# Taps' weights of a convolution read into one partition and spread over all 128 by TensorE

## Chip, cores, metric

One core of a Trainium2 chip runs the whole program. The metric is device time in microseconds, from the start to the end of the program, as a median over runs.

## What is computed

```python
# x [8, 4224, 192], weight [8 heads, 7 taps], all float32
w = exp(weight - max(weight)); w = w / (sum(w) + 1e-09)      # softmax over the 7 taps
y[b, s, h, g] = sum_k w[h, k] * x_pad[b, s + k, h, g]        # causal convolution, 24 columns a head
wq, wk = y @ moe_w_q, y @ moe_w_k                            # 192 -> 64
mixed = (wq @ wk^T / 8) @ y                                  # done as wq @ (wk^T y)
out = relu(mixed) @ moe_w_out                                # 192 -> 192
```

## The kernel before

There are 8 batches of 33 chunks of 128 rows. A batch of x is loaded in four pieces (five in batch 0) of 4 to 9 chunks by DMAs that GpSimd issues (`gen_load`, L543); they turn float32 into bfloat16 on the way, into a ring of three slots, so a load of batch b waits until the convolutions of batch b - 3 have read their slot. The convolution (`gen_conv`, L567) is a product with banded matrices `BAND` that hold the taps, 64 rows at a time; it runs in groups of chunks, five in batch 0 (one per piece) and two in each later batch, and each group in four pairs of heads. ScalarE or VectorE evicts each pair from PSUM into Y. VectorE transposes Y, TensorE makes the Gram matrix of Y and from it, with the weights `w_k`, the small matrix of the mix; `w_q` is applied to the transposed Y. Then come four units a batch: mix, `rl` and `rh` (relu into RT), `f_lo` and `f_hi` (the product with `w_out`), two output copies, and a store of 768 KB that SP issues.

Before all this lies the making of `BAND`. SP issues the load of the 8 x 7 weights (`load_w`, L359): 128 descriptors of 224 bytes, the same row on each of 128 partitions of WT_F. VectorE takes the maximum (`mx`, L441) and subtracts it (`sub`, L442), adds a mask for each partition's own tap (`mine`, L447), ScalarE takes the exponentials (`exp`, L457), VectorE sums them (`sm`, L458), takes the reciprocal (`rc`, L463), multiplies (`wn`, L464) and lays the products out (`taps`, L465). TensorE spreads them into two PSUM banks (`spread`, L478), and two copies (L498) bring them to BAND. Meanwhile TensorE runs filler products of 512 columns on zeros: four (`warm`, L421) that wait only for VectorE to have zeroed RUNUP, then a turn of the matrix `step` (`turned`, L426), then nine (`warm_2`, L430), which stand ahead of the spreading in its queue.

The other weights come by DMAs of SP: `w_out` (WF, L381) next after the taps, W32F (`load_32`, L378: `w_q` again, as 32 rows of 3 x 128), then `w_k` (L380) and `w_q` (L379), each in two DMAs. Four casts (L511) make W32 from W32F, one for each quarter of the partitions, on any of three engines; `casts_k` (L520) make among others the two halves of WKT, both on GpSimd, and `casts_q` (L515) one piece there.

The order is written out by hand in PLAN (L19): each entry is an operation's number (in the order in which the code adds them), its engine (P TensorE, A ScalarE, D VectorE, G GpSimd, S SP), a PSUM bank for a product, a variant, or, behind S, a second operation that SP waits for before it issues. Each engine takes its entries strictly in this order. Semaphore waits follow from what an operation needs (`Program.place`, L165).

Of the kernel before, what the change touches and what calls it, by code (L numbers as in the profile page):

```python
# [25 lines left out]
205P4 200P 206P 207D 202P0 201A 196P6 203P 197P 471G 131P3 204A 212P2 198D 132A 136P0 469G 137P3 139A 42D 148P6 150D  # L26
159P7 147P4 213P 43G 138A 149D 468G 214P 161A 372G 143P0 210D 144Pz 145A 140P3 371G 151P6 208D 152Px 141Px 153A 158P0x
215P 142D 160A 219P5 211D 154P3 155Px 283P0 156D 157S57 170P6 172A 284P 216P 220D 217P 285A 292P3 209D 286P6 293P 287P
218A 162P0 288D 294A 163Pz 223P5 164A 165P2 224D 166P 167D 298P4 169P0 171A 304P6 299P 295P2 300D 305P 296P 176P0y
# [188 lines left out]
def bass_lightweight_conv__then__hypermixer_token_mlp_kernel(  # L218
# [760 lines left out]
```

## Time and profile before

| | us |
|---|---|
| Median of 3 runs | 155.1 (153.89, 155.1, 156.55) |
| Profiled execution | 153.99 |
| Its span, first to last instruction | 152.1 |
| TensorE busy | 140.6 |
| VectorE busy | 119.5 |
| ScalarE busy | 110.6 |
| GpSimd busy | 31.0 |

The profiled execution is 1.9 us longer than its span, and stands 1.1 us below the median, close to the fastest of the three runs. Times in the rows below are counted from the start of the span. PE is TensorE, PEld its weight loads, DVE VectorE, ACT ScalarE, POOL GpSimd, SPq the DMA queue of SP; L345 and L329 are helpers that issue all products, so products are told apart by their tiles: `runup` is a filler, `ident,step` the turn, `taps,stept` the spreading, `xw,band` a convolution.

### The profile page before, as it was taken

To read this page: it belongs to the slowest core of one execution; us is meant where nothing else is said; L and a number is where in the kernel's file an instruction comes from. 1 tells how busy PE (TensorE), PEld (TensorE's weight loads), DVE (VectorE), ACT (ScalarE), POOL (GpSimd) and SP (SyncE) were. 2 spreads that over 40 slices of the span, in tenths; PEclk is the share of its full clock that TensorE was granted. 3 is DMA by queue.
4 is the path that set the end of the run, shared out by engine and by line. 5 is a ranking of instruction groups with operands and counts; after the bars stand their busy time and mean duration, and the time that the engine had idled before them with its cause. 6 is when DMAs were issued, how large, how long until landed. Compare 5 with 4: busy or idle time off the path is not lost.

```text
span 152.1 us, 5602 instructions
## 1 busy us (share of the span) xinstructions
PE 140.6 (92%) x2528; PEld 96.8 (64%) x2528; DVE 119.5 (79%) x165; ACT 110.6 (73%) x167; POOL 31.0 (20%) x41
## 2 busy tenths in 40 slices
PE   5977998999999999999999999999999999999920
PEld 2354745876666876785668766866667577965610
DVE  2659857998898898989988885899799978859500
ACT  0683648778768963798869886979399877989940
POOL 6935932900190007100360000000000000000000
PEclk9999999999999999999999999999999999999985
DMA  2999999999999999999999999999940899899994
GB/s 39 167 186 190 192 192 190 193 191 214 274 193 196 188 194 296 356 342 324 339 338 343 334 269 334 196 188 317 402 165 4 329 382 384 317 387 382 350 383 159
DMA packets 45336, 39.62 MB, mean 260 GB/s; under 512 B 35552, under 2 KB 37376, under 8 KB 45312
## 3 DMA queue, kind: packets, MB, share of 16 engines
q0 software_dynamic: 34320, 12.98, 71.4%
q1 hardware_dynamic: 10992, 26.28, 47.1%
q8 instruction: 20, 0.33, 0.8%
q14 instruction: 4, 0.03, 0.1%
HBM read 26.28 MB, written 25.95 MB: 343 GB/s over the span
## 4 chain that ended last, share of the span: by engine, by line
PE 77%; DMA 13%; DVE 2%; ACT 1%; POOL 1%; issue 1%; SPq 0%; POOLq 0%
PE ps L345 53%; PE ps L329 23%; DMA xw<-in_x_dram 10%; DMA wf<-in_moe_w_k_dram 3%; DVE out_sb L317 1%; PE ps L341 1%; ACT out_sb L317 1%; DVE rt L767 1%; POOL xw L550 1%; SPq L369 0%; POOL wkt L317 0%; POOL ident L402 0%; POOLq L402 0%; POOLq L964 0%
## 5 line engine op out<-in xcount | busy, mean ns | idle before, releaser
L550 POOL DMA_DIRECT2D xw<-in_x_dram x33 | 29.9, 919 | 42.6 <-PE ps L345 41.8
L766 ACT ACTIVATE rt<-ps 128x1024 bf16<-128x1024 f32 (+1 forms) x40 | 31.6, 826 | 6.7 <-PE ps L345 6.4
L345 PE MATMUL ps<-wol,rt 64*128 64x192 bf16 (+1 forms) x372 | 35.9, 246 | 0.0
L329 PE MATMUL ps<-xw,band 64*64 64x408 bf16 (+4 forms) x144 | 32.0, 303 | 2.5 <-DMA xw<-in_x_dram 0.5
L345 PE MATMUL ps<-xw,band 64*64 64x408 bf16 (+4 forms) x464 | 33.6, 316 | 0.0
L317 ACT CAST y<-ps 128x816 bf16<-128x816 f32 (+4 forms) x42 | 29.0, 705 | 6.3 <-PE ps L345 5.2
L317 DVE CAST y<-ps 128x768 bf16<-128x768 f32 (+4 forms) x34 | 28.9, 863 | 3.8 <-PE ps L345 3.3
L317 ACT COPY out_sb<-ps 128x768 f32<-128x768 f32 x36 | 28.5, 801 | 4.4 <-PE ps L345 3.6
L345 PE MATMUL ps<-y 128*64 128x64 bf16 (+1 forms) x528 | 30.8, 222 | 0.2 <-DVE y L317 0.2
L628 DVE STREAM_TRANSPOSE t<-y 128x768 uint32<-128x768 uint32 (+2 forms) x32 | 29.8, 959 | 1.4 <-ACT y L317 0.9
L345 PEld LDWEIGHTS ps<-y 128*64 128x64 bf16 (+1 forms) x528 | 26.0, 105 | 7.3 <-issue 6.3
L317 DVE COPY out_sb<-ps 128x768 f32<-128x768 f32 x28 | 26.6, 957 | 4.9 <-PE ps L345 4.0
L345 PEld LDWEIGHTS ps<-wol,rt 64*128 64x128 bf16 (+1 forms) x372 | 24.1, 115 | 3.0 <-ACT rt L766 0.9
L767 DVE TENSOR_SCALAR rt<-ps 128x512 bf16<-128x512 f32 (+1 forms) x24 | 21.5, 931 | 5.0 <-PE ps L345 4.9
L345 PEld LDWEIGHTS ps<-xw,band 64*64 64x64 bf16 x464 | 14.2, 103 | 12.4 <-issue 6.7
L345 PE MATMUL ps<-woh,rt 64*128 64x192 bf16 (+1 forms) x228 | 21.9, 253 | 0.1
L317 ACT CAST wqt<-ps 128x1024 bf16<-128x1024 f32 x12 | 11.8, 1014 | 11.7 <-PE ps L345 11.7
L345 PE MATMUL ps<-wqt,msb 64*64 64x512 bf16 (+1 forms) x133 | 16.9, 385 | 0.0
L326 PEld LDWEIGHTS <-band 64*64 64x64 bf16 x144 | 13.9, 105 | 3.2 <-issue 0.7
L345 PEld LDWEIGHTS ps<-woh,rt 64*128 64x128 bf16 (+1 forms) x228 | 12.9, 119 | 3.7 <-ACT rt L766 1.1
L329 PE MATMUL ps<-wol,rt 64*128 64x192 bf16 (+1 forms) x56 | 13.4, 246 | 0.2
L329 PE MATMUL ps<-wqt,msb 64*64 64x512 bf16 (+1 forms) x33 | 12.5, 384 | 0.0
(96 smaller groups left out, 118.8 us busy)
## 6 DMA issues: line engine op xcount, KB each, us to landing
out_dram<-out_sb SPq DMA_DIRECT2D x31, 768.0 KB, 8.0
xw<-in_x_dram POOLq DMA_DIRECT2D x24, 384.0 KB, 15.6
xw<-in_x_dram POOLq DMA_DIRECT2D x7, 432.0 KB, 15.2
out_dram<-outl SPq DMA_DIRECT2D x4, 192.0 KB, 5.3
out_dram<-out_sb SPq DMA_DIRECT2D x2, 384.0 KB, 4.9
xw<-in_x_dram POOLq DMA_DIRECT2D x1, 240.0 KB, 5.5
xw<-in_x_dram POOLq DMA_DIRECT2D x1, 192.0 KB, 5.0
wf<-in_moe_w_out_dram SPq DMA_DIRECT2D x1, 96.0 KB, 3.3
```

Of the source, the lines that this page charges most:

```text
L317: return lambda e, op: e.copy(dst(op), src(op)) if op.engine == "ACT" else e.tensor_copy(dst(op), src(op))
L326: e.ldweights(l, tile_position=place)
L329: return e.add_instruction(mybir.InstMatmult(name=nc.get_next_instruction_name(), engine=mybir.EngineType.PE, ins=[e.lower_ap(r), e.lower_ ...
L341: last = e.transpose(o, l, r)
L345: last = e.matmul(o, l, r, start=start, stop=stop, skip_group_check=True, tile_position=at[0] if at else None)
L550: "load", "POOL", lambda e, op: e.dma_start(dst, src), n * 128 * D * 4,
L628: lambda e, op: e.transpose(T[:, yb, c0 : c0 + n, :].rearrange("p c d -> p (c d)").bitcast(U32), Y[:, yb, c0 : c0 + n, :].rearrange("p c d ...
L766: return e.activation(dst(op), src(op), AF.Relu)
L767: return e.tensor_scalar(dst(op), src(op), 0.0, None, op0=ALU.max)
```

## The change

The load of the weights now puts one row of 224 bytes into one partition. A new memset on VectorE makes a row of 128 ones. A new product `on_all`, float32, one row deep, 128 by 56, lays the weights on all 128 partitions of a PSUM bank; it waits for the load and stands behind the turn of `step`. `mx` and `sub` read the weights there, and `sub` gives the bank back.

Two operations more shift the numbers in PLAN: 5 to 24 become 6 to 25, and all from 25 on rise by two. The order is for the most part the old one under new numbers. By engine, with old numbers, these entries moved:

- TensorE: `on_all` between the turn and the nine fillers; a few neighbours swapped (61 ahead of 59 and 76 in batch 0); in the last unit but one and the last, other variants of `f_lo` and `f_hi`, and the pair for the second half ahead of that for the first.
- VectorE: the zeroing of RUNUP is its first instruction, where it was the third. The zeroing of WKB moved from first place to batch 1. One of the four casts of W32F (old 40, new 42) stands between `mine` and `sm`; it stood behind the first eviction. The order around it is now `mx`, `own`, a memset, `sub`, two memsets, `mine`, cast, `sm`.
- The second copy to BAND went from VectorE to ScalarE. In the first two groups of batch 0 VectorE makes four evictions and ScalarE four, where ScalarE had six.
- Between the first 24 us and the last 12, sixteen pieces of work went from ScalarE to VectorE or the other way. In the last two units one large `rl` and two output copies went to VectorE and one output copy to ScalarE.
- GpSimd: loads 180, 181, 182, 183 (batch 1) and 279 to 282 (batch 2) in their natural order ahead of both casts of WKT (47, 46); they were 180, 181, 183, cast, 182, 281, 280, cast, 279. Loads of later batches swap places; five of them stand behind the cast of `w_q` (43), where three did.
- SP: `w_k` waits for the third load of batch 0 instead of the second, `w_q` for the first load of batch 2 instead of the second of batch 1. The first store to go out is that of the last chunks of batches 0 and 1, where it was one of batch 0.

```diff
@@ -17,46 +17,46 @@
 
 
 PLAN = """
-0S 13D 10D 4S 6D 18P4 53G 5D 1S 16G 17D 54G 22D 19P 25D 21P0 55G 26D 7D 20A 56G 23D 11D 27D 28A 8D 24D 57G 41A 9D 29D
-37A 30D 31D 180G 32D 33P1 52A 49A 34D 35P5 181G 58P6 3S54 36D 59P 60A 183G 76P0 70P2 61P4 77P 62P 63D 71P 78A 67P6
-79P0 72A 68P 40D 50A 64P2 80P 69A 73P4 81D 65P 74P 66A 85P6 75A 88P0 39A 91P2 86P 87D 82P4 92P 89P 83P 84A 122P7 14D
-90D 93D 94P0 100P2 119D 95P 101P 102A 103P5 104P 96D 97P0 105A 47G 118D 109P3 182G 98P 99D 110P 111A 106P5 123P 281G
-15D 120D 38A 112P2 51A 107P 115P0 108A 113P 116P 280G 114D 124P 117A 121D 45A 46G 125P 279G 126P 48D 2S181 133P0 135A
-134D 369G 282G 127P 190P4 370G 191P 193P2 128A 187P0 192D 194P 195A 184P6 188P 129P4 44D 12D 185P 189D 199P2 130A 186A
...
-803A 807S660 819P2 816Py 817D 821A 812P0 813Px 830P4x 823P2y 814A 818S749 824Py 825D 832A 826P6 827P 837P4 828A
-829S749 838P 834P6 839A 835Pz 841S 836A 840S750
+0S 7D 19P5 9D 4S 11D 55G 6D 5D 1S 17G 18D 56G 20P 23D 26P1 24D 22P0 27D 57G 25D 8D 21A 28D 58G 12D 10D 29D 30A 42D 31D
+59G 39A 32D 33D 182G 34D 35P7 40A 36D 37P5 38A 60P6 183G 50A 63P4 61P 62D 72P2 184G 78P0 73P 74A 79P 64P 69P6 80D 81P0
+65A 185G 70P 71A 66P2 75P4 82P 83D 3S57 67P 76P 87P6 68A 90P0 43D 281G 51A 93P2 77D 88P 89A 84P4 94P 91P 92D 85P 282G
+124P7 86A 95D 52A 96P0 41A 283G 102P2 121D 97P 54A 103P 53A 105P5 106P 104A 284G 98D 99P0 107A 15D 120D 111P3 100P
+101A 112P 108P5 125P 122D 113A 114P2 117P0 109P 110A 115P 118P 116D 126P 49G 119A 123D 127P 48G 372G 128P 46D 16D 14D
+135P0 137A 136D 373G 371G 129P 192P4 193P 195P2 194A 189P0 130D 196P 47D 190P 191D 186P6 197A 131P5 187P 132A 201P2
...
+818P 823D 814P0 815Px 816A 825P2 819D 820S660 832P4 826P 834A 828P0y 829Py 830D 827A 839P2y 831S749 836P5 837Px 838A
+842S562 840Py 841D 843S751
 """.split()
...
@@ -264,7 +264,8 @@
     def semaphore(name):
         return es.enter_context(nc.semaphore(name))
 
-    WT_F = sbuf("wt_f", [128, H, KC], F32)
+    WT_F = sbuf("wt_f", [1, H * KC], F32)
+    ONES = sbuf("ones", [1, 128], F32)
     WMX = sbuf("wmx", [128, H], F32)
     WEX = sbuf("wex", [128, 2, H, 8], F32)
     WSM = sbuf("wsm", [128, 2, H], F32)
@@ -358,8 +359,8 @@
 
     load_w = add(
         "load_w", "SP",
-        lambda e, op: e.dma_start(WT_F[:, :, :], bass.AP(w_t, 0, [[0, 128], [1, H * KC]])),
-        28000, dma=("w", semaphore("s_w"), 16), vt=-10)
+        lambda e, op: e.dma_start(WT_F[:, :], bass.AP(w_t, 0, [[H * KC, 1], [1, H * KC]])),
+        1000, dma=("w", semaphore("s_w"), 16), vt=-10)
 
     QS, KS, OS = slice(0, DH), slice(DH, 2 * DH), slice(2 * DH, 2 * DH + D)
 
@@ -383,6 +384,7 @@
     def dve(emit, ns, needs=(), vt=0.0, kind="setup"):
         return add(kind, "DVE", emit, ns, needs=needs, vt=vt, info={"ns": ns})
 
+    ones = dve(lambda e, op: e.memset(ONES[:, :], 1.0), 100, vt=-9.6)
     one = dve(lambda e, op: e.memset(IDENT[:, :], 1.0), 165, vt=-9.5)
     zero_r = dve(lambda e, op: e.memset(RUNUP[:, :].bitcast(U32), 0), 270, vt=-9.45)
     zero_s = dve(lambda e, op: e.memset(STEPT[:, :].bitcast(U32), 0), 130, vt=-8.9)
@@ -438,12 +440,22 @@
         lambda e, op: e.tensor_reduce(OWN[:, :], IDENT[:, :].rearrange("p (k i) -> p i k", i=16), AX.X, ALU.add),
         290, needs=[ident], vt=-8.92)
 
-    mx = dve(lambda e, op: e.tensor_reduce(WMX[:, :], WT_F[:, :, :], AX.X, ALU.max), 200, needs=[load_w], vt=-9.3)
-    sub = dve(
+
+    def spread_w(op):
+        yield bank(op.bank)[:, 0 : H * KC], ONES[:, :], WT_F[:, :], True, True, False
+
+    on_all = pe("setup", spread_w, needs=[load_w, ones], after=[turned], banks=1, vt=-9)
+
+    def w_all():
+        return bank(on_all.bank)[:, 0 : H * KC].rearrange("p (h k) -> p h k", k=KC)
+
+    mx = dve(lambda e, op: e.tensor_reduce(WMX[:, :], w_all(), AX.X, ALU.max), 230, needs=[on_all], vt=-9.3)
+    sub = add(
+        "setup", "DVE",
         lambda e, op: e.tensor_tensor(
-            WEX[:, 0, :, 0:KC], WT_F[:, :, :], WMX[:, :].unsqueeze(2).to_broadcast([128, H, KC]), ALU.subtract
+            WEX[:, 0, :, 0:KC], w_all(), WMX[:, :].unsqueeze(2).to_broadcast([128, H, KC]), ALU.subtract
         ),
-        210, needs=[mx], vt=-9.29)
+        230, needs=[mx], drains=on_all, vt=-9.29, info={"ns": 230})
     mine = dve(
         lambda e, op: e.tensor_tensor(
             WEX[:, 1, :, 0:KC], WEX[:, 0, :, 0:KC], OTHER[:, 0:KC].unsqueeze(1).to_broadcast([128, H, KC]), ALU.add
```

## Rows read from the trace of the kernel before

**Rows 1.** The page: busy us, share of the span, instructions of TensorE, VectorE, ScalarE.

```profile
PE 140.6 (92%) x2528; PEld 96.8 (64%) x2528; DVE 119.5 (79%) x165; ACT 110.6 (73%) x167; POOL 31.0 (20%) x41
```

**Rows 2.** The chain that ended last, to 24 us: start, us, what.

```profile
8.10 5.15 DMA wf<-in_moe_w_k_dram
...
13.55 10.21 DMA xw<-in_x_dram
...
23.80 0.32 PE ps L329
```

**Rows 3.** Busy time of each engine by stretch; behind it clock, DMA share, GB/s.

```profile
8.12:23.27 15.15, 13.76 (x307) 9.02 (x308) 11.22 (x22) 8.47 (x22) 7.60 (x10) 1.00 1.58 190
23.27:140.00 116.73, 115.46 (x2121) 82.26 (x2121) 101.69 (x122) 93.22 (x135) 16.54 (x19) 1.00 1.21 276
```

**Rows 4.** TensorE in order of time, 0 to 8.2 us: start, us, instruction, idle before.

```profile
1.53 1.89 PE L345 MATMUL ps<-runup 128*128 128x512 bf16 x4 [1.53 <-DVE runup L387]
3.21 0.31 PE L341 MATMUL ps<-ident,step 128*128 128x128 bf16 x1
3.31 3.94 PE L345 MATMUL ps<-runup 128*128 128x512 bf16 x9
7.18 0.51 PE L345 MATMUL ps<-taps,stept 112*64 112x64 bf16 x20
8.12 0.24 PE L329 MATMUL ps<-xw,band 64*64 64x120 bf16 x1 [0.43 <-DVE band L317]
```

**Rows 5.** VectorE in order of time, from 3.8 to 10 us.

```profile
3.87 0.21 DVE L441 TENSOR_REDUCE wmx<-wt_f 128x8 f32<-128x56 f32 x1 [0.72 <-DMA wt_f<-in_weight_dram]
4.12 0.22 DVE L443 TENSOR_TENSOR wex<-wt_f,wmx 128x56 f32<-128x56 f32 x1
...
5.58 0.29 DVE L459 TENSOR_REDUCE wsm<-wex 128x16 f32<-128x128 f32 x1
...
6.34 0.29 DVE L466 TENSOR_TENSOR taps<-own,wtap 128x128 bf16<-128x128 f32 x1
...
9.33 0.41 DVE L317 CAST y<-ps 128x240 bf16<-128x240 f32 x1 [0.87 <-PE ps L345]
9.77 0.35 DVE L317 CAST w<-w32f 32x384 bf16<-32x384 f32 x1
```

**Rows 6.** SP's DMA issues in order of time.

```profile
0.80 0.40 SPq L361 DMA_DIRECT2D wt_f<-in_weight_dram  x1
...
2.31 0.58 SPq L369 DMA_DIRECT2D w32f<-in_moe_w_q_dram  x1
...
19.11 0.85 SPq L369 DMA_DIRECT2D wf<-in_moe_w_q_dram  x2
```

**Rows 7.** DMA issues by tile: KB, us from issue to landing.

```profile
w32f<-in_moe_w_q_dram SPq DMA_DIRECT2D x1, 48.0 KB, 4.4
...
wt_f<-in_weight_dram SPq DMA_DIRECT2D x1, 28.0 KB, 3.0
```

**Rows 8.** ScalarE in order of time, around 7 and 10 us and in the tail.

```profile
6.69 0.51 ACT L317 CAST w<-w32f 32x384 bf16<-32x384 f32 x1 [1.22 <-DMA w32f<-in_moe_w_q_dram]
...
8.73 1.01 ACT L317 CAST y<-ps 128x240 bf16<-128x240 f32 x3 [0.54 <-PE ps L345]
...
10.14 0.84 ACT L317 CAST y<-ps 128x240 bf16<-128x240 f32 x3
...
143.67 2.51 ACT L317 COPY out_sb<-ps 128x768 f32<-128x768 f32 x3
```

**Rows 9.** L550, loads of x issued at 7.0 and 7.9: issue ns, landing us.

```profile
L550 POOL DMA_DIRECT2D xw<-in_x_dram x1: 943/943/943, 7.0 to 7.0; - x1
...
DMA to landing us min/median/max: 12.1/12.1/12.1
...
L550 POOL DMA_DIRECT2D xw<-in_x_dram x1: 923/923/923, 7.9 to 7.9; - x1
...
DMA to landing us min/median/max: 13.2/13.2/13.2
```

**Rows 10.** GpSimd in order of time: the load for batch 5 and its wait.

```profile
41.39 0.88 POOL L550 DMA_DIRECT2D xw<-in_x_dram  x1 [10.82 <-PE ps L345]
```

More of the change, by code (lines that the diff above doesn't have):

```diff
@@ L25 @@
-134D 369G 282G 127P 190P4 370G 191P 193P2 128A 187P0 192D 194P 195A 184P6 188P 129P4 44D 12D 185P 189D 199P2 130A 186A
[L26 to L29, printed above, removed]
@@ new lines @@
+188A 207P4 202P 203A 208P 209D 204P0 198P6 205P 199P 133P3 206A 214P2 2S281 200D 134A 138P0 139P3 141A 150P6 152D
+161P7 149P4 215P 140A 151D 216P 163A 145P0 212D 146Pz 147A 142P3 153P6 154Px 155D 143Px 144A 160P0x 217P 210D 162A
+221P5 156P3 157Px 45G 158A 285P0 13D 213D 172P6 286P 218P 471G 174D 44A 287A 219P 294P3 222D 288P6 472G 295P 211D 220A
+289P 296A 164P0 374G 290D 165Pz 225P5 166A 167P2 470G 168P 226D 169D 300P4 171P0 173A 306P6 473G 301P 297P2 302D 307P
+298P 178P0y 299A 308D 175P4y 179Py 176Py 180A 177D 227P3 223P2 291P6 303P0 224A 292P 293A 304P 562G 228D 375P4 305D
@@ new lines @@
+378P2 376P 379P 384P6 380A 276P0 377D 561G 385P 313P1 386A 309D 560G 229P2 230A 563G 277D 311D 314P 315P 231A 316P
+232P2 234A 233P7 235D 243P4 266P6 317P 318P 245D 255P7 268A 244P0 239P2 319A 240P 257A 236P4y 246D 241A 254P6x 237Py
+256D 250P0y 238A 251Py 247P2y 252A 265P4x 248Py 267D 258P6y 249A 261P0y 259Py 262Py 260A 278P3 312D 320P2 272P4y 263A
+279D 280S372 269P6y 273Py 321D 274A 270Py 271D 390P2 170S182 396P0 391P 181S184 397P 392A 381P4 474P6 398D 382P 475P
+387P2 383A 159S471 393P0 310D 388P 394P 662G 389A 322P5 476D 403P4 148S59 323A 404P 395A 661G 401D 264S185 324P0 325A
@@ new lines @@
+660G 402D 242S56 405P 659G 326D 406P 275S182 400D 327P2 329A 328P1 339P5 407P 330D 408P 338P6 361P0 409D 341A 350P1
+334P2y 340D 363A 331P4y 352A 335Py 332Py 333D 349P6x 336A 342P0 343Px 351A 345P2y 344D 360P4x 346Py 362A 353P6y 356P0y
+347D 354Py 357Py 358A 367P4y 355D 359S182 364P2y 368Py 365Py 366D 369A 414P1 410P0 495P6 337S56 489P4 415A 348S 411A
+496P 490P 399D 480P2 491A 416P0 412P1 481P 413D 483P4 417A 486P0 482A 497D 484P 487P 477P2 485A 488D 564P6 478P 749G
+565P 479A 567P4 492P0 566D 568P 493P 465P2 569A 751G 502P3 494D 466A 418P4 752G 419A 499D 750G 501D 503P 500D 504P
@@ new lines @@
+420A 498D 505P 421P0 423A 422P2 424D 432P4 433P6 444P7 506P 507P 434D 446A 428P0 508A 455P2 429P 435A 425P4y 457D 430A
+443P6x 426Py 427D 431S373 436P2y 445A 439P0y 437Py 440Py 438A 447P6 441D 509P5 448Pz 370S470 449A 450P2 253S59 510D
+451Pz 452D 511P1 573P4 512A 454P6 574P 456A 453S371 570P0 579P2 575D 571P 580P 585P6 572A 582P4 581D 586P 576P0 587A
+583P 584D 577P 461P2y 578A 458P6y 462Py 591D 459Py 463A 592P5 590D 460A 513P1 515A 588D 593P 594P 514A 595P 516P6 518A
+517P0 519D 527P1 528P3 596P 597P 529D 539P4 530A 550P0 523P6 598A 524P 541A 520P2y 552D 525A 538P4x 521Py 522D 534P0y
@@ new lines @@
+540A 531P6y 535Py 532Py 536A 542P4y 533D 549P2x 543Py 551A 545P0 544D 603P7 599P6 546Px 556P2y 600A 589D 553P4y 604A
+547A 548S 557Py 554Py 558D 663P6 555A 666P0 664P 667P 464S371 684P4 665D 668A 678P2 526S562 685P 679P 669P6 680D 686A
+672P0 670P 442S283 673P 671A 675P4 681P2 674D 676P 682P 605P6 559S752 677A 601P7 687D 691P0 683A 537S 692P 606A 602D
+690D 607P3 609A 688D 693P 608D 694P 689D 610P6 612A 611P3 621P4 644P1 695P 613D 696P 623D 622P2 646A 633P3 617P6 697A
+698P1 624A 618Px 635D 614P4y 699A 619A 632P0x 615Py 634D 625P2y 616A 620S661 628P6y 626Py 629Py 627A 643P4x 636P0y
```

35 lines of the change are left out of this document (7 added, 28 removed).

## The prediction

> **What bounds the kernel now.** I read the page first: TensorE is busy for 140.6 us, 92% of the span, and no other engine comes near [rows 1]. The reader should ask next where the other 8% lie, because only there can a change gain anything. The change sits in the first eight microseconds.
>
> The chain of waits, read in order of time, says what ends the head. It doesn't run through the taps' weights at all. It runs through a load of x: GpSimd issues the third piece of batch 1 at 13.55, that load lands 10.21 us later, and TensorE starts the second convolution group of batch 1 at 23.80 [rows 2]. The table by stretch shows what follows: from the first convolution (8.12) to 23.27, where TensorE has used up what it has, it is busy for 13.76 of 15.15 us; then it waits 0.53 us for that load (23.27 to 23.80); up to 140 it is busy for 115.46 of 116.73, that wait among the 1.27 us it is not [rows 3]. The reader should take from this that a microsecond saved before 8 us is worth only what reaches the restart at 23.80, and that whatever moves the restart moves the end with it, one to one.
>
> Next, TensorE's own timeline of the head. Four filler products run from 1.53, the turn of `step` at 3.21, nine more fillers from 3.31 for 3.94 us, then the spreading of the taps at 7.18 and the first convolution at 8.12 [rows 4]. The nine take 3.94/9 = 0.44 us each for 512 columns, which is the 1.2 GHz level, and the spreading starts as the last one ends. VectorE's timeline beside it: the maximum `mx` starts at 3.87, on the landing of the weights; the sum `sm` at 5.58; the taps are made from 6.34 and done at 6.63 [rows 5]. So in the kernel before the taps were ready half a microsecond ahead of TensorE. The fillers, not the weights, started the spreading.
>
> **The change part by part.**
>
> *The DMA.* It was issued at 0.80 [rows 6] and landed 3.0 us later [rows 7], at 3.8. With one row in place of 128 it lands no later than 3.8. How early is not shown; the lower bound is its issue's own end, 1.2. [...] I take 3, inside the bounds; up to the turn's end at some 3.5 nothing in the sum hangs on it. At 3.8 the product below would wait 0.3 us, and the fillers behind it would end at 8.0 instead of 7.4.
>
> *The spreading product `on_all`.* TensorE gets it after the turn (3.21, 0.31 us long) and before the nine fillers. Its price is not in the trace; the nearest rows bound it: 0.1 us or so if it merely follows the pipeline, as the first filler follows the turn by 0.10, and 0.44 for a product of 512 columns [rows 4]. I take 0.25, since 56 columns in float32 lie nearer the small end. The Trainium skill, FP8 and Floating Point Precision, section TensorE Precision Notes, says that true FP32 makes four passes through the array; the sum by it is 4 x 56 = 224 columns, an estimate of 0.19 us at the fillers' rate, so it speaks against the change only mildly. The nine fillers behind it then run from about 3.5 and end at 3.5 + 3.94 = 7.4, where they ended at 7.25. Alone that would be +0.2 on the first convolution.
>
> *Reading PSUM.* `mx` and `sub` take 0.21 and 0.22 us each now; the plan's own figures are a little more. I add 0.05 in all, and it is hidden behind the next point.
>
> *A cast moved on VectorE.* This is the one that costs. In the new order VectorE has one of the four casts of W32F (0.35 us, at 9.77 now) between `mine` and `sm`. VectorE takes its queue in order, so `sm`, `rc`, `wn` and `taps` stand behind it, and TensorE's spreading behind them. The cast waits for the DMA of W32F, issued at 2.31 [rows 6] and landing 4.4 us later [rows 7]; ScalarE's cast of the same tile starts at 6.69, straight on that landing [rows 8]. Now the bounds of the landing in the new kernel. Late: 6.69, as now. Early: 2.31 + 3.0 = 5.3, as the taps' 128 rows took with nothing ahead of them. Between: ahead of W32F in the same queue lie 28 KB of taps and 144 KB of `w_out`; the queue, 220 KB with W32F, runs from issue 0.80 to 6.69, so dropping 28 KB is worth 28/220 of some 4.9 us, 0.6 us. I take 6.1. Then: cast to 6.5, and from the start of `sm` to the end of `taps` 6.63 - 5.58 = 1.05, so 7.55. The spreading starts at 7.6 instead of 7.18 and the first convolution at about 8.5: +0.4 (bounds +0.2, where the fillers rule, and +1.0 at a landing of 6.69, which also covers fillers that end at 8.0).
>
> *Evictions shared out.* In the first two groups of batch 0, ScalarE now makes six of eight evictions, three from 8.73 and three from 10.14 [rows 8], and VectorE sits idle 0.87 us before its first [rows 5]; the new order gives each four. An eviction there costs 0.41 on VectorE [rows 5] and about a third of 1.01 on ScalarE [rows 8], so between 0 and 0.4 us comes back before the third group; I take half, 0.2. TensorE reaches the restart at 23.27 + 0.4 - 0.2 = 23.47.
>
> *Loads reordered.* GpSimd issues the third piece of batch 1 ahead of the fourth and all of batch 2 ahead of the two casts of `wkt`; the DMA of `w_k` waits for the third load instead of the second, that of `w_q` for a load of batch 2 instead of one of batch 1. The restart needs the third and the fourth piece, so their swap changes nothing. What matters is `w_q`: it was issued at 19.11 [rows 6], into the middle of this pair. The second piece of batch 1 landed at 7.0 + 12.1 = 19.1 and the fourth at 7.9 + 13.2 = 21.1 [rows 9], 2.0 apart, and the third at 13.55 + 10.21 = 23.76 [rows 2], 2.6 later for the same size. Without `w_q` between them, the pair is in at 23.2 (best) to 23.76 (if something else filled the gap). I take 23.3. The restart is the later of 23.3 and 23.47: 23.5 instead of 23.80, so -0.3.
>
> *What hides the rest.* `w_q` is now issued behind the first load of batch 2, some 2.2 us after the pair, at about 25.5; with the 5.15 us that the like DMA of `w_k` took [rows 2] it is in at 30.7. Queued behind its GpSimd cast are five loads for batches 3 and 4, and behind those the loads of batch 5. They go out some 4 us later than now. The cover is GpSimd's own idle time: having issued all of them it sat idle for 10.82 us up to 41.39, waiting for a slot of x to come free [rows 10]. So I cost the delay at nothing; if the cover were gone, each microsecond beyond those 10.8 would cost one.
>
> *The tail.* ScalarE makes the last three output copies in a row, 2.51 us from 143.67 [rows 8], 0.84 each. The new order gives two of the last four to VectorE, so that the very last can run side by side, but it also moves one of the last large `rl` from ScalarE to VectorE and puts the last `f_lo` behind another product. The bounds are one copy either way, -0.8 and +0.8; I take 0, because a gain behind TensorE's end and a loss ahead of it are both in the edit.
>
> The sum: -0.3 on the profiled execution's 153.99, so 153.7. The runs shown have a median of 155.1, 1.1 above that execution; the same step from there gives 154.8. I name 154.2, between the two.
>
> **The rivals.**
>
> *Blocked VectorE.* W32F lands at 6.69 as now. First convolution +1.0, evictions give back 0.2, so TensorE reaches the restart at 23.27 + 0.8 = 24.1, 0.3 behind now: 153.99 + 0.3 = 154.3, and 154.8 on my scale, which stands 0.5 above the profiled execution. For it: the landing sits behind x in the engines too. Against: fewer rows ahead.
>
> *The tail gains.* The two last copies run side by side and the full 0.8 is kept, on top of -0.3: 154.2 - 0.8 = 153.4. For it: ScalarE's three copies in a row. Against: the moved `rl`.
>
> *The clock comes late (slower).* Place: `on_all` stands in front of the nine fillers and waits for a DMA, which the fillers didn't. If the weights land at 3.8 or later, TensorE idles before them, and the 1.2 GHz level of the fillers could last into the convolutions. The first time it lasted from 1.53 to about 7; as long again, 5.5 us, means 2.75 us of work lost, less the 0.53 of slack: +2.2 against now: 153.99 + 2.2 + 0.5 = 156.7. It decides from a low stretch of about 1 us behind 8.5, and beyond 2% from some 8 us. Against it: one row should not land later than 128.
>
> *The order costs elsewhere.* Sixteen pieces of ScalarE's and VectorE's work change engine between 24 and 140. TensorE's 1.27 us of gaps show how tight this is [rows 3]; one badly placed is worth up to a copy, 0.84, of wait, on top of -0.3: 155.0. For it: there is no slack left in that stretch. Against: the two engines swap one piece for another.
>
> **How the numbers follow.** Forecast (-0.7 to 0) 0.45; blocked VectorE 0.22; tail 0.13; late clock 0.08; order elsewhere 0.12. Within 2% is about what a measurement can tell from no change; nearly all cases fall there. Faster by over 2% would need 3 us out of a head that holds only 0.53 us of waiting: 0.02. Slower by over 2%: the long end of the clock and of the order: 0.06. Same: 0.92. The range takes the tail's gain with the lower scale, 153.7 - 0.8 = 152.9, less 0.2 for the bounds of the restart, 152.7; above, the late clock without its far end, 156.7.
>
> **What would show it.** Right: the cast of W32F on VectorE waits for its DMA near 6 and `sm` starts behind it; spreading near 7.6, first convolution near 8.5; the wait for x before the restart shrinks below 0.3; the middle stays as long. Wrong: a restart later than 23.8, a gap of TensorE between the turn and the fillers, or a last copy that ends 0.5 us nearer to or farther from the restart than now.

## The result and the profile after

The changed kernel takes 156.38 us (median of 4 executions, 156.15 to 158.09), the kernel before 154.74 beside it: a ratio of 1.015, 95% interval 1.011 to 1.019. It is inside the forecast's range and inside 2%, but some 1.6 us slower where 0.3 to 0.9 faster was forecast. The profiled execution took 156.55, its span 154.8. A ratio leaves out executions more than 1.5% above their kernel's fastest, so it need not be that of the medians, and the traces of h4 and i3 below are of such executions.

TensorE's order of time, the answer to [rows 4]: start, length, instruction, idle before.

```profile
3.01 0.29 PE L342 MATMUL ps<-ident,step 128*128 128x128 bf16 x1
3.23 0.67 PE L346 MATMUL ps<-wt_f,ones 1*128 1x56 f32 x2
3.83 3.33 PE L346 MATMUL ps<-runup 128*128 128x512 bf16 x9
8.38 0.51 PE L346 MATMUL ps<-taps,stept 112*64 112x64 bf16 x20 [1.22 <-DVE taps L478]
9.32 0.24 PE L330 MATMUL ps<-xw,band 64*64 64x120 bf16 x1 [0.43 <-DVE band L318]
```

The product that lays the weights on all partitions follows the turn without a wait, so its DMA was in time. The fillers end at 7.16, near the forecast's 7.4. Then TensorE stands idle for 1.22 us until the taps come, and the first convolution starts at 9.32 instead of 8.12. VectorE beside it, against [rows 5]:

```profile
3.94 0.22 DVE L452 TENSOR_REDUCE wmx<-ps 128x8 f32<-128x56 f32 x1 [0.51 <-PE ps L346]
...
6.31 0.94 DVE L318 CAST w<-w32f 32x384 bf16<-32x384 f32 x1 [1.01 <-DMA w32f<-in_moe_w_q_dram]
7.28 0.28 DVE L471 TENSOR_REDUCE wsm<-wex 128x16 f32<-128x128 f32 x1
...
8.04 0.29 DVE L478 TENSOR_TENSOR taps<-own,wtap 128x128 bf16<-128x128 f32 x1
```

The cast ahead of `sm` waits 1.01 us for its load, as the forecast said it would; but then it takes 0.94 us, where the same cast took 0.35 [rows 5]. The table by stretch, from the first convolution to the end of the work at hand, from there to 140, and then two slices of four microseconds (the last three columns: granted clock, DMA share, GB/s; before: [rows 3]):

```profile
9.32:25.34 16.02, 15.32 (x307) 10.17 (x308) 11.26 (x21) 9.77 (x23) 7.29 (x10) 0.79 1.58 190
25.34:140.00 114.66, 113.69 (x2090) 81.21 (x2088) 95.65 (x115) 94.55 (x137) 15.71 (x18) 1.00 1.19 271
...
8.00:12.00 4.00, 3.02 (x88) 2.29 (x89) 1.92 (x7) 1.81 (x6) 4.00 (x5) 0.72 1.51 175
12.00:16.00 4.00, 3.64 (x56) 2.60 (x55) 3.02 (x5) 2.87 (x8) 1.35 (x2) 0.50 1.57 191
```

The first stretch lasts 16.02 us instead of 15.15. The granted clock was 1.00 when the spreading began, fell to 0.50 (1.2 GHz) at 9.75, behind the 1.22 us of idle, and came back at 16.57; before, it stayed at 1.00. TensorE is out of work at 25.34 and restarts at 25.50 (before: 23.27 and 23.80). From 60 to 130 the same products run 2.05 us later than before, unchanged. Then the tail:

```profile
146.48 0.27 PE L346 MATMUL ps<-woh,rt 64*128 64x192 bf16 x2 [0.78 <-ACT out_sb L318]
...
147.78 0.80 ACT L318 COPY out_sb<-ps 128x768 f32<-128x768 f32 x1 [1.36 <-PE ps L346]
...
147.95 0.96 DVE L318 COPY out_sb<-ps 128x768 f32<-128x768 f32 x1 [1.26 <-PE ps L346]
```

The last two copies do run side by side, but TensorE waited 0.78 us just ahead of them; the last copy ends at 148.91, 2.73 later than before's 146.18 [rows 8], 0.7 more than the middle. GpSimd, the answer to [rows 10]:

```profile
32.92 0.29 POOL L318 CAST wqh<-wf 64x128 bf16<-64x128 f32 x1 [11.71 <-DMA wf<-in_moe_w_q_dram]
33.32 4.55 POOL L562 DMA_DIRECT2D xw<-in_x_dram  x5
43.33 1.76 POOL L562 DMA_DIRECT2D xw<-in_x_dram  x2 [5.46 <-PE ps L346]
```

It now waits for `w_q` first (11.71 us) and still has 5.46 us left before the next slot comes free: the late `w_q` cost nothing.

### The profile page after: what moved, and what is told of

It is laid out like the page before. It is cut to its first block, busy times and chain, and to the rows that moved or that the text cites. A ratio compares the mean times of both kernels' runs of the same rounds, so it can differ in the third digit from the quotient of the medians.

```text
span 154.8 us, 5607 instructions
## 1 busy us (share of the span) xinstructions
PE 142.4 (92%) x2532; PEld 98.5 (64%) x2532; DVE 118.3 (76%) x163; ACT 113.0 (73%) x170; POOL 31.1 (20%) x41
## 4 chain that ended last, share of the span: by engine, by line
PE 74%; DMA 11%; POOL 4%; DVE 3%; ACT 2%; issue 2%; POOLq 0%; ACTq 0%
PE ps L346 51%; PE ps L330 22%; DMA xw<-in_x_dram 11%; POOL xw L562 4%; DVE out_sb L318 2%; ACT y L318 2%; PE ps L342 1%; DVE rt L779 1%; ACT out_sb L318 1%; POOL ident L404 0%; ACT msb L714 0%; POOLq L404 0%; ACT rt L778 0%; ACTq L210 0%; POOLq L976 0%
## 5 line engine op out<-in xcount | busy, mean ns | idle before, releaser
L318 ACT CAST y<-ps 128x816 bf16<-128x816 f32 (+4 forms) x45 | 31.7, 719 | 5.6 <-PE ps L346 4.3
L330 PE MATMUL ps<-xw,band 64*64 64x408 bf16 (+4 forms) x146 | 33.5, 315 | 1.7 <-DVE y L318 0.5
L346 PE MATMUL ps<-xw,band 64*64 64x408 bf16 (+4 forms) x462 | 34.9, 331 | 0.0
L318 ACT COPY out_sb<-ps 128x768 f32<-128x768 f32 x38 | 30.0, 802 | 6.0 <-PE ps L346 5.4
L778 ACT ACTIVATE rt<-ps 128x1024 bf16<-128x1024 f32 (+1 forms) x38 | 30.0, 826 | 5.3 <-PE ps L346 5.0
L346 PE MATMUL ps<-y 128*64 128x64 bf16 (+1 forms) x528 | 31.5, 224 | 0.0
L318 DVE COPY out_sb<-ps 128x768 f32<-128x768 f32 x26 | 24.6, 956 | 7.2 <-PE ps L346 6.6
L779 DVE TENSOR_SCALAR rt<-ps 128x512 bf16<-128x512 f32 (+1 forms) x26 | 23.4, 932 | 8.5 <-PE ps L346 8.4
L318 DVE CAST y<-ps 128x768 bf16<-128x768 f32 (+4 forms) x31 | 25.6, 843 | 5.0 <-PE ps L346 4.3
L346 PEld LDWEIGHTS ps<-xw,band 64*64 64x64 bf16 x462 | 15.1, 109 | 12.0 <-issue 5.9
L327 PEld LDWEIGHTS <-band 64*64 64x64 bf16 x146 | 15.0, 112 | 3.2 <-issue 0.9
```

The costliest lines, as they stand in the source:

```text
L318: return lambda e, op: e.copy(dst(op), src(op)) if op.engine == "ACT" else e.tensor_copy(dst(op), src(op))
L327: e.ldweights(l, tile_position=place)
L330: return e.add_instruction(mybir.InstMatmult(name=nc.get_next_instruction_name(), engine=mybir.EngineType.PE, ins=[e.lower_ap(r), e.lower_ ...
L346: last = e.matmul(o, l, r, start=start, stop=stop, skip_group_check=True, tile_position=at[0] if at else None)
L778: return e.activation(dst(op), src(op), AF.Relu)
L779: return e.tensor_scalar(dst(op), src(op), 0.0, None, op0=ALU.max)
```

## The experiments

Theories: (1) the wait of the moved cast sets the head; (2) the new matmul, or reading PSUM, costs; (3) the loads' or the stores' order costs; (4) the tail costs. Each run stands beside the kernel before on its own chip. The last three columns are read from one trace of each: start of the first convolution, the restart (TensorE's first convolution of the second group of batch 1), both in us, and packets of x moved between 3 and 4 us.

| kernel | median us (n) | ratio [95%] | conv | restart | packets |
|---|---|---|---|---|---|
| before | 154.4 to 154.7 | 1 | 8.12 | 23.80 | 74 |
| after | 156.38 (4) | 1.015 [1.011, 1.019] | 9.32 | 25.50 | 162 |
| f1 new code, old order | 154.70 (10) | 1.002 [0.998, 1.005] | 8.35 | 23.65 | 79 |
| f2 old code, new order | 156.88 (4) | 1.015 [1.007, 1.023] | 9.32 | 25.38 | 73 |
| e4 before, cast moved | 156.73 (4) | 1.011 [1.006, 1.017] | 9.85 | 25.44 | 75 |
| e1 cast back | 155.96 (10) | 1.006 [1.002, 1.011] | 7.75 | 24.64 | 143 |
| h4 W32F's load first | 155.93 (6) | 1.012 [1.007, 1.016] | 7.76 | 24.63 | 313 |
| e6 twelve fillers | 157.32 (4) | 1.018 [1.014, 1.022] | 9.33 | 26.79 | 227 |
| e3 loads back | 157.15 (4) | 1.012 [1.004, 1.020] | 9.32 | 24.79 | 142 |
| e2 tail back | 157.07 (4) | 1.015 [1.009, 1.021] | 8.65 | 24.51 | 190 |
| g1 cast and stores back | 155.19 (10) | 1.002 [0.999, 1.005] | 7.90 | 23.41 | 80 |
| h1 stores back | 155.18 (10) | 1.005 [1.002, 1.008] | 8.68 | 24.22 | 83 |
| h2 cast back, w_k, w_q early | 156.49 (10) | 1.006 [1.001, 1.011] | 7.68 | 24.80 | 140 |
| g2 cast, stores, tail back | 155.48 (12) | 1.007 [1.004, 1.011] | 8.33 | 24.37 | 85 |
| i1 before, new stores | 154.48 (10) | 1.000 [0.997, 1.003] | 7.67 | 23.80 | 75 |
| i2 g1 with late stores new | 154.90 (10) | 1.003 [1.000, 1.006] | 7.98 | 24.10 | 79 |
| i3 g1 with early stores new | 158.86 (4) | 1.021 [1.013, 1.028] | 7.70 | 27.27 | 128 |
| i4 h4 and stores back | 155.78 (12) | 1.006 [1.003, 1.010] | 8.76 | 24.18 | 310 |
| j1 after, two last waits | 155.89 (12) | 1.007 [1.004, 1.010] | 8.74 | 24.21 | 84 |
| j2 i3, two last waits | 156.08 (5) | 1.008 [1.003, 1.012] | 7.70 | 24.27 | 96 |

One trace is one execution. `after` and e2 differ only in the order of the last two units, and so do g1 and g2; yet their restarts lie 0.99 and 0.96 us apart. Behind the first pair stand the length of one cast (0.94 and 0.35 us) and of a low clock (6.83 and 3.41 us), behind the second the clock again, which fell to 0.50 at 10.37 in g2 and not in g1. So a difference of a microsecond between two restarts shows nothing by itself; the times decide.

### Code or order

f1: the new load, product and reads with the whole old PLAN, renumbered; in each engine's order only the memset of ones (5D) and `on_all` (26P1) come in.

```diff
-0S 13D 10D 4S 6D 18P4 53G 5D 1S 16G ... 19P 25D 21P0 ...
+0S 14D 11D 4S 7D 19P4 55G 6D 1S 17G ... 5D 18D 23D 20P 26P1 27D 22P0 ...
```

> The new load, memset and product, with the old order under new numbers: nothing else moved, so the cast of W32F is back behind the first eviction, the loads, casts and the tail are as before. Theory A (the order costs, not the product): the product before the nine fillers delays the spreading by 0.2 to 0.6 us, which the 0.53 us wait for x at the restart takes up; 154.5 to 155.0, a ratio to before of 0.999 to 1.002. Theory B (the product itself costs): the taps reach VectorE later or the fillers break, first convolution near 9.3 as in the changed kernel, 156.0 or more, ratio 1.008 and up.

f2: the kernel before with the new PLAN, numbers moved down.

```diff
-0S 13D 10D 4S 6D 18P4 53G 5D 1S 16G 17D 54G 22D 19P ...
+0S 6D 18P5 8D 4S 10D 53G 5D 1S 16G 17D 54G 19P 22D ...
```

> The old load on 128 partitions and no product, with the new order in all else: the cast of W32F ahead of the sum, the loads and stores rearranged, the new tail. Theory A (the order costs): first convolution at 9.3 or later, TensorE idle for about 1 us ahead of the spreading, last copy 0.7 us farther from the restart; 156.0 to 157.0, ratio 1.009 to 1.016. Theory B (the product costs): near before, 154.5 to 155.2, ratio below 1.004.

f1 takes the time of the kernel before (154.70), f2 that of the changed one (156.88). So the code is free in the old order, and the carried-over order, or what comes with it, costs all of the 1.5%. Theory 2 falls. f2's spreading starts where the changed kernel's does:

```profile
8.38 0.59 PE L344 MATMUL ps<-taps,stept 112*64 112x64 bf16 x20 [2.12 <-DVE taps L465]
```

Its moved cast starts at 6.58 and takes 0.67 us, the granted clock is 0.50 from 8.65 to 15.48, and x moves as before (73 packets).

### The cast

e4: before, with one edit, the cast of W32F ahead on VectorE.

```diff
-... 28A 8D 24D 57G ... 68P 40D 50A ...
+... 28A 57G ... 183G 40D 8D 24D ... 68P 50A ...
```

> The kernel before, whole, with one edit: the cast of W32F, 40D, moved on VectorE from behind the first evictions to just ahead of op 24, behind op 11 and 27. Theory one (the cast's wait for its load, at the head of VectorE, is what cost the head): the spread starts 0.9 to 1.3 us later than before's 7.18, the first conv matmul at about 9.0 to 9.4, TensorE idles a microsecond and its clock falls to 1.2 GHz somewhere in 8 to 16 us; the restart comes 1 to 2 us after before's 23.80, and the time is 155.7 to 156.7. Rival (the loads' and stores' order carried over does it, the cast alone is harmless): spread and first conv within 0.3 us of before's, no fall of the clock, and 154.6 to 155.1.

VectorE and TensorE of e4 in order of time:

```profile
6.37 0.89 DVE L316 CAST w<-w32f 32x384 bf16<-32x384 f32 x1 [1.21 <-DMA w32f<-in_moe_w_q_dram]
...
8.91 0.51 PE L344 MATMUL ps<-taps,stept 112*64 112x64 bf16 x20 [1.55 <-DVE taps L465]
```

156.73, ratio 1.011: moved alone, the cast does most of the damage (f2, the same code with the whole new order: 1.015). In the old order three more small operations stood behind it, so the spreading came even later, at 8.91; the clock fell at 10.72 for 3.41 us.

e1: the changed kernel with this cast behind the first eviction.

```diff
-... 30A 42D 31D 59G ... 62D 72P2 ...
+... 30A 31D 59G ... 62D 42D 72P2 ...
```

> The changed kernel with one entry moved: the cast of W32F on VectorE goes from ahead of the sum to behind VectorE's first eviction. Theory A1 (this one cast makes the head late): spreading at about 7.3 to 7.5, first convolution about 8.4, no low stretch of the clock; TensorE reaches the restart at about 23.5 instead of 25.3. If TensorE's lateness alone set the restart, the gain is 1.5 to 1.8 us: 154.6 to 154.9. Theory A2 (the late load sets it as well: the fourth piece of batch 1 landed at 25.41 with fifteen of its sixteen parts in at 23.31): TensorE now waits at the restart, gain 0.2 to 0.5 only: 155.9 to 156.2.

The first convolution is back at 7.75, but the restart only at 24.64, and the time at 155.96. TensorE now waits 1.4 us for pieces of x instead, and a new stall of 0.82 us appears at 68.75:

```profile
68.75 0.27 PE L345 MATMUL ps<-woh,rt 64*128 64x192 bf16 x1 [0.82 <-issue]
```

"issue" means that TensorE waited for nothing that the profile shows. A fetch of 16 KB of instructions, at 62.70 in the kernel before, starts at 66.35 here; that it makes the stall is inferred from these times. e2 and e3 have the same stall (0.81 at 68.62, 0.82 at 69.15). In `after` the fetch starts at 66.44 and there is none, presumably because TensorE is a microsecond later there anyway. So in e1 and e2 the stall took back what an earlier head had gained: counted against the kernel before, e1's products go from 0.92 us late to 1.93, e2's from 0.80 to 1.99, those of `after` only from 1.94 to 2.05.

h4: on SP the load of W32F ahead of that of `w_out`.

```diff
-0S ... 4S ... 1S ...
+0S ... 1S 4S ...
```

> The changed kernel with one swap on SP: the load of W32F is issued ahead of the load of w_out, so it lands 0.5 to 2 us earlier; the cast stays ahead of sm. Theory one (the cast's wait for its load costs the head, 1.0 us of idle VectorE): the idle before the cast shrinks by as much as the landing moves, the spread starts at 7.2 to 7.8, TensorE idles under 0.6 us for the taps, no fall of the clock before 16 us, and the time is 155.3 to 156.0, near that with the cast put back (155.96). Rival (the cast's own time and its place in the queue cost, not the wait): spread still at 8.1 or later, time 156.2 to 156.8.

VectorE of h4:

```profile
5.33 0.35 DVE L317 CAST w<-w32f 32x384 bf16<-32x384 f32 x1
```

With the load in early the cast at the same place has no wait, takes 0.35 us, and the convolution starts at 7.76 as with the cast put back. The wait is thus what delays the head, not the place. The time fell by half a microsecond only (155.93, ratio 1.012), which is not clear of noise: in the profiled execution, its longest at 159.05, stalls near 68 us cost another 3.5 us, one of them 1.93 us of issue.

e6: three more fillers, so that TensorE stays busy until the taps.

```diff
-    warm_2 = pe("run_up", run_up(9), after=[turned], banks=1, vt=-8.9)
+    warm_2 = pe("run_up", run_up(12), after=[turned], banks=1, vt=-8.9)
```

> The changed kernel with twelve filler matmuls instead of nine in the run-up, so that TensorE is busy until the taps are there. Theory one (the 1.2 us in which TensorE idles for the taps makes its clock fall, and the low stretch has a price of its own): no fall at 9.75, TensorE free of its first work before the restart at 24.3 to 24.7 instead of 25.34, with the first conv still at about 9.3. The later stall for instructions near 68.7 us takes part of that back, so the time is 155.6 to 156.2. Rival (the low stretch is covered by the wait for loads, only the delay counts): the clock stays up and the restart is still at 25.3 to 25.5, time 156.2 to 156.6.

Stretches of e6:

```profile
12.00:16.00 4.00, 3.10 (x64) 1.93 (x60) 3.19 (x8) 3.40 (x9) 1.46 (x2) 1.00 1.55 188
16.00:20.00 4.00, 2.92 (x40) 2.19 (x43) 1.91 (x2) 0.95 (x3) 1.47 (x3) 0.62 1.59 191
```

The clock stays at 1.00 past 16, and still the restart is at 26.79: x comes late, TensorE waits 1.1 us for it, and the clock falls at 16.96. The time, 157.32, is above both expectations. Keeping the clock up to that point didn't win the time back; pieces of x that come later are a second cause here.

### Loads and tail

e3: GpSimd's order and the waits of `w_k` and `w_q` as before.

```diff
-... 182G 183G 184G 185G 281G 282G 283G 284G 49G 48G ...  3S57 2S281
+... 182G 183G 185G 49G 184G 283G 282G 48G 281G 371G ...  3S56 2S183
```

> The changed kernel with GpSimd's whole order and the waits of w_k and w_q on SP as before; cast, compute and other stores as changed. Theory one (the cast's wait sets the head, the loads' order adds little): spread 8.2 to 8.5, first conv 9.1 to 9.4, the restart 25.0 to 25.6, time 156.1 to 156.6. Rival (the order of the loads is what costs: the third piece of b0 lands about 1 us late, and the fourth of b1 with it): third piece of b0 at 10.0 instead of 10.9, restart at 24.0 to 24.5, time 155.0 to 155.8.

Head as changed (9.32), third piece of batch 0 still late (11.41 us; before 10.03), time 157.15. Putting the loads' order back brings nothing.

e2: the last two units' order as before.

```diff
-812A 824A 835A 805A 816A 834A 827A 838A   808D 823D 819D 830D 841D
+812A 835A 824A 805A 823A 816A 834A 830A 841A 838A   808D 819D 827D
```

> The changed kernel with the last two units as before: the products' variants and sequence, who evicts what, and the waits of the last stores. Theory T (the tail costs by itself): the last copy ends 2.0 us behind before's instead of 2.7, gain 0.7 us: 155.7. Rival (the tail only follows the late head, and its length depends on where the last stores' neighbours stand): no gain, 156.4.

The last copy ends 1.91 us behind before's, the middle runs 1.99 behind, so the tail's 0.7 is gone; yet the time is 157.07. The stall at 68.62 had taken back what this execution's earlier restart gave. g2 below, with the old tail too, is no faster than g1 (155.48 and 155.19). The trace shows the tail's 0.7 us; that it is worth anything, the times don't show. It stays open.

### The stores

The first entries of SP's list, new against old (the number behind S is an operation awaited):

```diff
-0S 4S 1S 3S57 2S281 280S372 170S182 181S184 159S471 148S59 264S185 242S56 275S182 359S182 337S56 348S 431S373 ...
+0S 4S 1S 3S56 2S183 159S59 280S373 148S57 242S184 275S 181S182 170S182 348S58 264S 359S184 337S185 253S283 ...
```

g1 is e1 with the old list, h1 the changed kernel with it, g2 is g1 with the old tail; h2 is e1 with 3S56 and 2S183 alone.

> The changed kernel with the cast of W32F put back behind the first eviction (as in e1) and the whole order of SP's queue, the stores above all, as before. Theory one (in the new order of the stores an instruction fetch comes late, and TensorE stalls 0.82 us at 68.75): the fetch is at about 62.7 again, there is no issue stall near 68.7, the shift against before stays at 0.9 to 1.0 from the restart to 140 us, and with the tail's 0.7 the time is 155.0 to 155.5. Rival (the stall comes from the order of compute, not the stores): the stall is there as in e1, shift 1.8 to 1.9 from 68.7, time 155.8 to 156.2.

> The changed kernel with SP's whole order (w_k, w_q and the stores) as before; the cast stays ahead of sm. Theory one (the cast's place sets the head, the stores' order adds a late stall that a kernel already two microseconds late doesn't show): spread at 8.2 to 8.5, first conv 9.2 to 9.4, clock falls between 8 and 16 us, the shift in the middle is 1.3 to 2.1 and the time 156.0 to 156.7, as with the cast moved alone (156.73). Rival (the stores' order was the larger part of the cost): time 154.9 to 155.5.

> The changed kernel with the cast back behind the first eviction, and of SP's order only the waits of w_k and w_q as before; the stores stay as changed. Theory one (the stores' order delays the instruction fetch): the fetch that came at 62.7 before comes at 66 to 67, and TensorE stalls 0.5 to 0.9 us near 68.7 with nothing to wait for, if the restart is less than 1.5 us late; shift 0.8 to 1.9 from there, time 155.4 to 156.0. Rival (the waits of w_k and w_q made the difference between e1 and g1): fetch at 62.7, no stall, third piece of b0 landed by 10.0, time 154.9 to 155.4.

> The changed kernel with the cast, SP's whole order and the last two units' order as before; the other orders of compute and GpSimd's order stay as changed. Theory one (cast, stores and tail are all that the new order costs): shift within 0.4 us of before all through, last copy at 145.8 to 146.4, time 154.2 to 154.8, and by 0.1 to 0.6 less than with the tail as changed (155.19). Rival (the tail's 0.7 is given back in the last store, or belongs to other orders): 155.0 to 155.4.

With the old list g1 is at 155.19 and h1 at 155.18, 0.8 and 1.2 us below e1 and after (by the ratios 0.4% and 1.0%; the first is not clear of noise, the second is); `w_k` and `w_q` alone (h2) bring nothing. With the old list the moved cast costs little: h1, which has it ahead, is at 1.005, g1 at 1.002. But the difference lies where no store runs. In g1 the third piece of batch 0 lands at 9.44, in e1 at 11.29, and the restart is at 23.41 against 24.64. The first store of results goes out behind 33 us.

So the list was split: i1 puts the new stores into the kernel before, i2 and i3 put their late part (from the twelfth) and their early part into g1.

In i2 the list is the old one to 337S185 and the new one from 431S373. In i3 it is the old one to 2S183, the new one from 280S372 to 348S, and the old one from 253S283.

> The kernel before with the changed kernel's order of the stores on SP, and nothing else; w_k and w_q keep their places. Theory one (the stores' order costs by itself, by the late instruction fetch): fetch at 65 to 67 instead of 62.7, TensorE stalls 0.5 to 0.9 us near 68 with nothing to wait for, shift 0 before 66 and 0.5 to 0.9 after it, time 155.0 to 155.6. Rival (it acts by the loads' pace in the first 11 us): the third piece of b0 lands 0.5 us or more after before's 10.03 and the restart comes 0.5 to 1.2 us later. Rival two (the stores' order costs nothing in the kernel before): 154.3 to 154.8 with neither.

> As g1 (cast and SP's whole order back), but the stores from the twelfth on, all issued after 66 us, in the changed order. Theory one (only the first eleven stores, which meet the fetch at 62.7, cost): fetch at 62 to 63, no stall near 68, third piece of b0 landed by 10.2, time as g1, 154.9 to 155.4. Rival (the late half costs, by something that isn't its own time, since it can't reach back to the loads): third piece of b0 at 10.8 or later, time 155.7 to 156.5.

> As g1, but the first eleven stores, issued before 66 us, in the changed order, and the later ones as before. Theory one (these meet the fetch): fetch at 65 to 67, stall of 0.4 to 0.9 us near 68, no change ahead of 60 us, time 155.6 to 156.2. Rival (loads' pace): third piece of b0 at 10.8 or later and restart 0.5 us or more after g1's 23.41, with or without the stall.

In the kernel before the new stores cost nothing (1.000), and in the new code the late ones next to nothing (1.003). The early eleven go with 2%: third piece at 11.87, convolution at 7.70, restart at 27.27. All of that lies ahead of the first of these stores (57.8 us). Theory 3, as a matter of waits, falls.

i4 joins h4's swap and the old list: 

> The changed kernel with SP's order as before except that W32F's load is issued ahead of w_out's; the cast stays ahead of sm, where it then has no wait (as in h4). Theory one (the wait at the head and the stores' order are what the change cost): cast at 5.3 for 0.35 us, spread at 6.8 to 7.0, restart 23.2 to 23.9, no stall near 68, time 154.3 to 155.2. Rival (the rest of the new order, loads on GpSimd and tail, costs too): 155.3 to 156.0.

155.78: no stall near 68, but x again slow in the head (third piece at 10.85), and nine fillers that ran to 7.8 because the clock rose only at 7.91. At 1.006 it is no better than h1 (1.005), which has only the old list.

### The length of SP's program

The trace counts 70 instructions of SP in every kernel of the new code with the new early stores, 72 in those with the old ones; some entries of the old list need a wait of their own. So two more waits, on a store long done, were put behind everything (the trace then counts 71, one more than without):

```diff
+        for _ in range(2):
+            e.wait_ge(S_OUT[0], program.count["o0"])
         e.nop()
```

j1 is the changed kernel with them, j2 is i3 with them.

> The changed kernel, every order as it is, with two more waits on a store that is long done, behind all else on SP: 72 instructions on SP as in h1, against 70. Theory one (the program's size decides how the first loads run, the stores' order doesn't): x packets in the fourth microsecond 75 to 90 instead of 162, the third piece of b0 at 9.4 to 10.3, time 155.0 to 155.8, as h1 (155.18). Rival (the order of the stores decides): 140 or more packets, third piece at 10.8 or later, time 156.2 to 156.8.

> The kernel i3 (cast back, first eleven stores in the changed order, the others as before) with the same two waits behind all else on SP. Theory one (program's size): x packets in the fourth microsecond 75 to 90 instead of 128, third piece of b0 at 9.4 to 10.3 instead of 11.87, time 154.8 to 155.8. Rival (order of the stores): as i3, third piece at 10.8 or later, time above 157.

The queue of x (packets, MB, share) of after, from 3 to 4 us and from 5 to 10:

```profile
q0 software_dynamic: 162, 0.06, 63.7%
...
q0 software_dynamic: 2000, 0.75, 136.6%
```

The same of j1:

```profile
q0 software_dynamic: 84, 0.03, 31.8%
...
q0 software_dynamic: 2400, 0.90, 153.4%
```

SP's first issues in after:

```profile
1.20 0.93 SPq L370 DMA_DIRECT2D wf<-in_moe_w_out_dram  x2
2.17 0.58 SPq L370 DMA_DIRECT2D w32f<-in_moe_w_q_dram  x1
```

And in j1:

```profile
1.22 0.96 SPq L370 DMA_DIRECT2D wf<-in_moe_w_out_dram  x2
2.22 0.58 SPq L370 DMA_DIRECT2D w32f<-in_moe_w_q_dram  x1
```

Two waits that run behind 148 us changed how the DMAs of the first ten microseconds run: SP's issues come 0.02 to 0.05 us later, x starts more slowly and then moves 2400 packets instead of 2000 between 5 and 10 us, the third piece lands at 9.74 instead of 10.89. The ratio goes from 1.015 to 1.007 for after (the medians by 0.5 us) and from 1.021 to 1.008 for i3; in both the intervals lie apart, on at most four executions of after and of i3. All eight kernels of the new code with 70 show 128 packets or more in the fourth microsecond; of those with 72 or with the two waits all but i4, which issues W32F first, show 96 or fewer. The third piece of batch 0 divides them the same way: 10.29 to 11.87 us in the eight, 9.44 to 10.20 in the others, again but for i4 (10.85). Kernels of both sorts stood side by side on four chips; j1 and j2 ran on a fifth by themselves. It isn't the count as such: f2 and i1, the old code with 70 and 69, show 73 and 75. How a program's length reaches these DMAs, no run here shows.

In `after` the late x itself cost TensorE only 0.2 us of waiting. What j1's trace has in its place is the cast, which starts 0.06 us earlier and is 0.59 us shorter, and the clock:

```profile
6.25 0.35 DVE L318 CAST w<-w32f 32x384 bf16<-32x384 f32 x1 [0.96 <-DMA w32f<-in_moe_w_q_dram]
```

j1's stretch from first convolution to the end of the work at hand:

```profile
8.74:24.06 15.32, 13.71 (x307) 8.79 (x308) 11.20 (x21) 9.56 (x23) 7.99 (x11) 1.00 1.59 191
```

No fall of the clock, 0.7 us shorter than after's 16.02, and from 60 to 130 a steady 0.73 us behind the kernel before. This trace is of j1's fastest execution (154.52; its median is 155.89).

## Why the prediction was wrong

**Right.** The frame, nearly: most of what matters happens ahead of the restart and in the tail. That the restart moves the end one to one is not quite so: a restart 1.70 us late became 2.05 by 60 us in after, 0.41 became 0.73 in j1, and 0.15 early became 0.03 late in f1, so the shorter wait there didn't last. f1's load and product put the first convolution 0.23 us later and cost nothing, as costed; `w_q` was covered. In after the rival "order elsewhere" found nothing: between 30 and 138 us TensorE's only wait over 0.12 us is one of 0.24, which the kernel before has too (in e1, e2 and e3 the stall near 68 us is such a place). And the named culprit was the right one: alone, in e4, the cast costs 1.1%.

**The cast, mis-sized.** Forecast: landing 6.1, cast to 6.5, first convolution +0.4, at most +1.0. Measured: start 6.31, end 7.25, +1.2. Of the 0.8 missing, 0.2 is the landing and 0.6 is the cast's own length, for which the row with 0.35 [rows 5] was taken although GpSimd was then not issuing loads. (The sum of the landing also has a slip: from 0.80 to 6.69 is 5.9 us, not 4.9; with 5.9 it gives 5.9, and the miss grows to 0.4.) Five casts that started at 6.31 to 6.58 (after, e3, e4, e6, f2) all ended between 7.24 and 7.26; three that started at 6.20 to 6.26 (e2, h1, j1) took 0.35. GpSimd's pair of load issues around it, first in after, where VectorE waits (shortest, median, longest ns; first and last start):

```profile
L562 POOL DMA_DIRECT2D xw<-in_x_dram x2: 948/983/1018, 6.1 to 7.0; - x2
```

then in e2, where GpSimd does:

```profile
L561 POOL DMA_DIRECT2D xw<-in_x_dram x2: 908/996/1083, 6.0 to 7.1; - x2
```

Whoever comes first goes on and the other waits. The Trainium skill, SBUF — State Buffer, section Who interferes with whom, says just that: a cast on VectorE that uses both its ports and GpSimd exclude each other, and the order of issue decides who blocks. The trace agrees: 0.6 us for VectorE or 0.1 us for GpSimd. GpSimd's issue began at 6.04 to 6.06 in all eight, ahead of every cast; so it stands in the cast's way only from some 0.2 to 0.85 us into it (an estimate: 6.26 and 6.31 are the starts on either side, 7.25 less 0.35 the end). Which way it goes hung on 0.05 us of W32F's landing: after and e2, with the same head, fell on different sides. The conflict was to be had before the run, and it speaks against this edit.

**The product, mis-sized without effect.** `on_all` took 0.67 us in two records, outside the 0.1 to 0.44 given; the fillers behind it ended in time all the same (7.16). That was luck of the clock, which rose at 6.33: in i4, where it rose at 7.91, they held the spreading to 7.78 with the taps done at 6.76.

**The stretch to the restart: the step that failed most.** The forecast let the evictions give 0.2 back and had the pair of loads in at 23.3. Measured, the stretch is 0.87 longer and the last of the pair landed at 25.41. The late pair cost only a wait of 0.15. Behind the stretch stands the granted clock, 0.79 on average: f2, low as long and with x at its usual pace, has 15.9. j1, without a fall, still takes 15.32, g1 15.33 and h1 15.38, where the forecast's 15.15 - 0.2 would be 14.95: nothing came back from the evictions. So the wait of 0.53 us before the restart, from which the forecast took its gain, was all used up: in j1 the restart is at 24.21, in after at 25.50, forecast 23.5. Of j1's 0.7, 0.24 is the first convolution, 0.37 the stretch and the rest a wait of 0.15 for an eviction.

**The rivals.** "Blocked VectorE" is nearest in mechanism, but its 154.8 lacked the length of the cast. "The clock comes late" happened in another form: the clock was up in time and fell again, in after behind TensorE's idle time for the taps, not for `on_all`. Its price was too high. It took half of the low time; measured, with 3.41 us of it the stretch to the restart took 15.45 in e4 against before's 15.15, and 15.31 in e3 against j1's 15.32, so 0.3 at most; with 6.83 us, 0.7 in after and 0.6 in f2, against j1.

**The tail.** Costed at 0 within 0.8; the last copy came 0.7 later in the trace, at TensorE's wait for ScalarE's copy (0.78). Its worth in time stays open.

**The sum.** Of after's 1.5%, 0.8 goes with the length of SP's program (after against j1), which no step of the forecast could have named; 0.7, some 1.0 us, stays in j1, and its trace shows 0.73 of that, from the head. That doesn't make the slow x the cause of the 0.8: f2 loses the same 1.5% with x at its usual pace, by the long cast and the low clock, and those are what j1's trace lacks. How much of the 0.8 is the cast, how much the clock and how much x stays open, as does the way from two last waits to a landing in the first 7 us.

## What to carry to other kernels

Before an instruction that waits for a DMA is moved ahead on an in-order engine, list all that then stands behind it, and price it by rows in which the same neighbours are at work, not by its quiet ones: 0.35 us became 0.94, and 1.0 of waiting came on top. If two versions differ ahead of the first edit that could act, pad the program's end before looking for a cause in the order: two idle waits took away a third of this loss by the medians, half by the ratios. And an order that was worked out for one set of lengths is a change by itself; test code and order apart first.

## What was not expected of the hardware

- Two waits of SP at the end of a program changed the pace of the loads in its first 10 us (2000 against 2400 packets between 5 and 10 us), and with them 0.8% here and 1.3% in i3 by the ratios.
- A fetch of 16 KB of instructions takes mostly 0.9 to 1.0 us in these traces (up to 1.9). Begun 3.65 us later than before (66.35 for 62.70 in e1), it was followed by 0.8 us in which TensorE waited for nothing that the profile names; that it then lacked instructions is inferred. The Trainium skill, Runtime: NRT & Kernel Launch, section Instruction fetch mechanics, calls the crossing mostly hidden; of the 20 fetches in each trace here, this one was not in e1, e2 and e3.
- One row of 224 bytes was there 1.2 us behind its issue (issue 0.80, the trace's completion 2.01), 128 rows of the same 3.0 [rows 7].
- The granted clock's rise after the run-up came anywhere from 4.6 (i1) to 7.9 us (i4) in kernels whose first microseconds are alike, and the nine fillers took 2.6 (i3) to 4.0 us (i4) by it. Over whole executions of the kernel before the mean clock ran from 0.961 to 0.993, so a single trace's clock need not be that kernel's own.
